# The 32 stores of converted weights, issued from GpSimd's queue instead of SyncE's

## The chip, the cores and the metric

The kernel runs on one core of a Trainium2 chip. The time is that of one execution on the device, in microseconds (us). The core has five engines that run in parallel, each through its own list of instructions in order: TensorE (PE: matmuls and transposes; its weight loads are shown as PEld), VectorE (DVE), ScalarE (ACT), GpSimd (POOL) and SyncE (SP, which here only issues DMAs). The engines meet at semaphores. DMAs move data between the chip's memory and the on-chip memory on 16 DMA engines that all queues share.

## The reference

Three layers follow each other, on 2 x 576 tokens with 8 heads of 64:

```
scores = scale * q @ k^T                       # per batch and head, 576 x 576
kth    = 32nd largest score of each row
attn   = softmax(where(scores >= kth, scores, -1e9))
x      = attn @ v                              # as 1152 tokens x 512
h      = x @ w_in                              # 512 -> 2048
x      = (max(h,0) + log1p(exp(-|h|))) @ w_out # 2048 -> 512
h      = x @ w_in2
out    = (max(h,0) + alpha * min(h,0)) @ w_out2
```

The four weight matrices come as 64-bit floats and have to be made into 32-bit floats on the chip.

## The kernel before

The 1152 tokens are nine tiles of 128 rows. `CHUNKS` puts them into five chunks of one or three tiles (tiles 3, 4, 5, then 6 to 8, then 0 to 2). Attention works by rows of one tile and one head, 72 in all. For a row PE makes the scores (`pss`, L471), ACT copies them to `s` (L476), DVE finds the 32 largest in four rounds of MAX8 and MATCH_REPLACE8 (L480, L483), ACT marks what lies below the 32nd (`e`, L509), POOL subtracts the mark from the scores in two halves of 288 columns (L514), and ACT takes the exponential (L516). PE turns `e` (L529, L535) and multiplies by v (`pav`, L557). The two feed-forward layers go over 16 blocks of 128 hidden columns, `up` (`ph`) and `down` (`pa`), for each chunk or group of chunks. In the small chunks the matmuls take 32-bit floats as they are (L652, L698); in the others each product is three products of high and low parts (L624 to L626).

The weights of a layer are 16 units of 128 x 1024: eight pairs of blocks for `up` and eight for `down`. The first use of a unit is `convert`: two loads of 512 KB from the input (L348) into a raw buffer `cr` of which there are two (`RAWB`), two DVE operations (L351, L354), one ACT operation for each half (L357), and four additions of 128 x 256 on POOL (L360). The result lies in `cx`, one of 15 slots of a ring that also holds the weights loaded later. Then `cx` is stored to a scratch tensor `ws` in the chip's memory (L364, 512 KB). A later chunk loads it from there (`w<-ws`, L386). So there are 32 stores for two layers: 16 fall between 17 and 135 us, 16 between 194 and 335 us.

The order on every engine is written out by hand: `ORDER` is a table of the numbers of all operations, and each is emitted when its number comes up. A word `f5` stands for five filler matmuls (`scrap`, L789) on PE. An operation waits for what wrote what it reads, and for what read or wrote what it overwrites. The loads of a unit (L348) wait for the last L360 of the unit that had the raw buffer before, and in the table the store of that unit follows soon after them.

Of the kernel before, what the change touches and what calls it, by code (L numbers as in the profile page):

```python
# [8 lines left out]
F32 = mybir.dt.float32  # L9
# [94 lines left out]
class Schedule:  # L104
# [10 lines left out]
    def op(self, engine, emit, reads=(), writes=()):  # L115
        me = len(self.ops)
        earlier = set()
        for x in reads:
            wrote, read = self.state.setdefault(getattr(x, "key", x), [None, []])
            if wrote is not None:  # L120
                earlier.add(wrote)
            read.append(me)
        for x in writes:
            entry = self.state.setdefault(getattr(x, "key", x), [None, []])
            earlier.update(entry[1])
            if entry[0] is not None:
                earlier.add(entry[0])
            entry[0], entry[1] = me, []
            self.owner[getattr(x, "key", x)] = x
        for x in reads:  # L130
            assert self.owner.get(getattr(x, "key", x), x) == x
        earlier.discard(me)
        self.ops.append((emit if isinstance(engine, tuple) else (emit,), earlier))
# [160 lines left out]
def pieces(n, size):  # L294

    return [slice(a, min(a + size, n)) for a in range(0, n, size)]
# [3 lines left out]
def topk_attention_moe_kernel(ctx: ExitStack, tc: tile.TileContext, q, k, v, w1, w2, w3, w4, alpha, out):  # L300
    nc = tc.nc
# [4 lines left out]
    op = plan.op  # L306

    def buf(tag, bufs, shape, dtype, name):
        return plan.buffer(sb, tag, bufs, shape, dtype, name)

    def bank(tag, bufs, n, name):
# [11 lines left out]
       writes=["rest"])  # L323
# [12 lines left out]
    def slot(tag, bufs, dtype, name, unit=None):  # L336
        x = Halves(buf(tag, bufs, [P, WIDE], dtype, name))
        lies[x.whole.key] = unit
        return x

    def convert(unit):
        layer, j, m = unit
        nm = f"{layer}{m}{j}"
        f = slot("wring", RING, U32, f"cx{nm}", unit)
        raw = Halves(buf("craw", RAWB, [P, WIDE, 2], U32, f"cr{nm}"))
        source = mats[layer][m][j].bitcast(U32)
        for part in raw.parts:
            op("SP", lambda part=part: nc.sync.dma_start(  # L348
                part().rearrange("p a b -> p (a b)"), source[:, 2 * part.lo:2 * part.hi]), writes=[part])
        high = lambda: raw()[:, :, 1]  # L350
        op("DVE", lambda: nc.vector.tensor_scalar(  # L351
            f().bitcast(U32), high(), 3, 0x3FFFFFF8, op0=ALU.logical_shift_left, op1=ALU.bitwise_and), reads=raw.parts,
           writes=f.parts)
        op("DVE", lambda: nc.vector.tensor_scalar(  # L354
            high(), high(), 0xC0000000, None, op0=ALU.bitwise_and), reads=f.parts, writes=raw.parts)
        for part, r in zip(f.parts, raw.parts):
            op("ACT", lambda r=r: nc.scalar.activation(  # L357
                r().bitcast(I16)[:, :, 2], r()[:, :, 0], AF.Copy, scale=2.0 ** -29), reads=[part], writes=[r])
            for cs in pieces(DM, 256):
                op("POOL", lambda part=part, r=r, cs=cs: nc.gpsimd.tensor_add(  # L360
                    part().bitcast(I32)[:, cs], part().bitcast(I32)[:, cs], r().bitcast(I32)[:, cs, 1]), reads=[r],
                   writes=[part])
        z = dr.tile([P, WIDE], F32, tag=f"ws{nm}", name=f"ws{nm}")
        op("SP", lambda: nc.sync.dma_start(z, f().bitcast(F32)), reads=f.parts, writes=[f"ws{nm}"])  # L364
        scratch[unit] = z
        return f

# [10 lines left out]
    def fetch(unit, no, ci, whole):  # L378
        fresh = unit not in scratch
        if whole and unit in ready and lies.get(ready[unit][0].whole.key) == unit:  # L380
            return
        if fresh:
            x = convert(unit)
        else:
            x = slot("wring", RING, F32R, f"w{no}", unit)
            op("SP", lambda: nc.sync.dma_start(x().bitcast(F32), scratch[unit]),  # L386
               reads=["ws%d%d%d" % (unit[0], unit[2], unit[1])], writes=x.parts)
        ready[unit] = (x,)
        if whole:
            return  # L390
        hi = slot("wring", RING, F32R, f"wh{no}")
        lo = slot("wring", RING, F32R, f"wl{no}") if fresh else x
        op("ACT", lambda: nc.scalar.copy(hi(), x().bitcast(F32)), reads=x.parts, writes=hi.parts)  # L393
        for l, a, h in zip(lo.parts, x.parts, hi.parts):
            low_piece(l, lambda a=a: a().bitcast(F32), h, [h, a] if fresh else [h], [l])
        ready[unit] = (hi, lo)
# [445 lines left out]
```

## Time and profile before

| | |
|---|---|
| median of 3 runs | 664.43 us (663.53 to 664.88) |
| the profiled execution | 661.64 us |
| its span, from the first to the last instruction | 659.8 us |
| busy PE, DVE, ACT, POOL | 643.9, 542.9, 496.9, 377.0 us |
| bytes moved by DMA | 98.46 MB, mean 149 GB/s |
| DMAs issued by SP | 67 `w<-ws`, 64 `cr`, 32 `ws<-cx`, and q, k, v, alpha and the output |

The busy shares are means over stages with different limits. Rows of a timeline give start and duration in us; in brackets stands the idle time of the engine just before the instruction, and who ended it. The row of a DMA on SPq is its issue; when its data has landed stands in a view of its own.

### The profile page before, as it was taken

How to read it: one execution, taken by the hardware profiler on the slowest of the kernel's cores; microseconds unless marked ns; L12 is line 12 of the kernel's file. 1: busy time of each engine (PE TensorE's matmuls, PEld its weight loads, DVE VectorE, ACT ScalarE, POOL GpSimd, SP SyncE). 2: the span in 40 equal slices, each digit the busy share in tenths (PEclk: the TensorE clock that was granted, in tenths of full speed). 3: DMA queues.
4: the chain of work that ended last, by engine and by line, in shares of the span. 5: the costliest groups of instructions: out<-in, count | busy, mean ns of one | idle time of the engine just before them, and what ended most of it. 6: DMA issues, size and time to landing. Idle time of an engine off the chain costs nothing.

```text
span 659.8 us, 12350 instructions
## 1 busy us (share of the span) xinstructions
PE 643.9 (98%) x4330; PEld 500.2 (76%) x4330; DVE 542.9 (82%) x1046; ACT 496.9 (75%) x1118; POOL 377.0 (57%) x402
## 2 busy tenths in 40 slices
PE   9999997999999899999999999999999999999997
PEld 7899765667677555555567788779898999999886
DVE  5999999999999999999998889999734654664632
ACT  4878898998799988788788889888545667673432
POOL 2566765642343677887585769886644343742520
PEclk9999999999999999999999999999999999999999
DMA  8765777740044379858424222221243433432501
GB/s 298 257 212 210 242 253 241 241 164 1 1 136 137 112 217 311 290 167 266 155 80 147 94 97 96 65 97 58 79 133 125 146 118 129 160 128 96 160 1 48
DMA packets 30159, 98.46 MB, mean 149 GB/s; under 512 B 3473, under 2 KB 4241, under 8 KB 30097
## 3 DMA queue, kind: packets, MB, share of 16 engines
q1 hardware_dynamic: 29952, 97.54, 45.2%
q8 instruction: 34, 0.56, 0.4%
q14 instruction: 29, 0.23, 0.1%
q10 hardware_dynamic: 144, 0.13, 0.1%
HBM read 78.52 MB, written 19.14 MB: 148 GB/s over the span
## 4 chain that ended last, share of the span: by engine, by line
PE 87%; issue 4%; POOL 3%; ACT 2%; DMA 2%; DVE 1%; SPq 0%; POOLq 0%; DVEq 0%
PE ph L652 11%; PE pa L698 10%; PE scrap L789 9%; PE ph L624 7%; PE pa L624 7%; PE ph L626 7%; PE ph L625 7%; PE pa L625 7%; PE pa L626 7%; PE pss L471 6%; PE pp L529 4%; POOL cx L360 2%; DMA cr<-in_w_dram 2%; POOL e L514 1%; PE pav__3750 L557 1%
## 5 line engine op out<-in xcount | busy, mean ns | idle before, releaser
L370 POOL TENSOR_TENSOR w<-w,wh 128x512 fp32r<-128x512 f32 x82 | 126.3, 1550 | 101.4 <-ACT wh L393 93.8
L514 POOL TENSOR_TENSOR e<-s,e 128x288 f32<-128x288 f32 x144 | 121.0, 860 | 64.4 <-ACT e L509 58.6
L480 DVE MAX8 m<-r 128x8 f32<-128x576 f32 x216 | 155.7, 747 | 0.1
L360 POOL TENSOR_TENSOR cx<-cx,cr 128x256 int32<-128x256 int32 x128 | 94.1, 762 | 62.2 <-ACT cr L357 60.5
L483 DVE MATCH_REPLACE8 r<-m,r 128x576 f32<-128x576 f32 x144 | 106.4, 742 | 0.0
L698 PE MATMUL pa<-cx,g 128*128 128x512 f32 x188 | 92.9, 604 | 2.3 <-DVE g L666 2.3
L357 ACT ACTIVATE cr<-cr 128x512 int16<-128x512 uint32 x64 | 82.5, 1378 | 4.4 <-DVE cr L354 4.0
L393 ACT CAST wh<-w 128x1024 fp32r<-128x1024 f32 x64 | 66.8, 1045 | 6.3 <-PE pa L624 2.0
L476 ACT COPY s<-pss 128x288 f32<-128x288 f32 x144 | 53.3, 407 | 21.7 <-PE pss L471 21.2
L480 DVE MAX8 m<-s 128x8 f32<-128x576 f32 x72 | 52.8, 749 | 10.6 <-ACT s L476 10.5
L789 PEld LDWEIGHTS scrap<-ident 128*128 128x128 f32 x474 | 55.9, 195 | 6.7 <-issue 5.3
L789 PE MATMUL scrap<-ident 128*128 128x128 f32 x474 | 59.5, 282 | 1.4 <-POOL ident masks.py:199 1.4
L516 ACT ACTIVATE e<-e,nb 128x576 f32<-128x576 f32 x72 | 55.8, 776 | 5.7 <-POOL e L514 5.5
L624 PE MATMUL pa<-w,gh 128*128 128x512 f32 x144 | 59.0, 409 | 0.0
L371 DVE TENSOR_TENSOR w<-w,wh 128x512 fp32r<-128x512 f32 x46 | 37.2, 811 | 26.4 <-ACT wh L393 24.8
L625 PE MATMUL pa<-wh,gl 128*128 128x512 f32 x144 | 56.8, 395 | 0.0
L626 PE MATMUL pa<-wh,gh 128*128 128x512 f32 x144 | 56.8, 395 | 0.0
L670 ACT ACTIVATE g<-ph 128x384 f32<-128x384 f32 x48 | 23.4, 490 | 43.7 <-PE ph L626 37.7
L471 PE MATMUL pss<-ks,q 64*64 64x288 f32 x576 | 53.1, 432 | 2.5 <-ACT pt L532 2.2
L672 DVE SCALAR_TENSOR_TENSOR g<-g,rest,ph 128x384 f32<-128x384 f32 x48 | 29.2, 608 | 31.8 <-ACT g L670 31.7
L371 DVE TENSOR_TENSOR gl<-g,gh 128x384 fp32r<-128x384 f32 x41 | 42.2, 1029 | 15.2 <-ACT gh L679 14.8
L652 PEld LDWEIGHTS ph<-xh,cx 128*128 128x128 f32 x336 | 42.0, 191 | 15.8 <-issue 8.2
(131 smaller groups left out, 1461.6 us busy)
## 6 DMA issues: line engine op xcount, KB each, us to landing
w<-ws SPq DMA_DIRECT2D x67, 512.0 KB, 3.3
cr<-in_w_dram SPq DMA_DIRECT2D x64, 512.0 KB, 5.5
ws<-cx SPq DMA_DIRECT2D x32, 512.0 KB, 6.6
v<-in_v_dram SPq DMA_DIRECT2D x12, 320.0 KB, 6.3
ks<-in_k_dram SPq DMA_DIRECT2D x11, 288.0 KB, 5.1
q<-in_q_dram SPq DMA_DIRECT2D x8, 256.0 KB, 5.3
out_dram<-o SPq DMA_DIRECT2D x8, 256.0 KB, 2.5
ks<-in_k_dram SPq DMA_DIRECT2D x2, 144.0 KB, 2.4
```

What stands on the lines that cost most here:

```text
L360: op("POOL", lambda part=part, r=r, cs=cs: nc.gpsimd.tensor_add(part().bitcast(I32)[:, cs], part().bitcast(I32)[:, cs], r().bitcast(I32)[: ...
L370: lambda: nc.gpsimd.tensor_sub(lo(), x(), hi().bitcast(F32)),
L471: nc.tensor.matmul(pss[n]()[part], qr()[head, pair, part], ks()[head, cs], start=True, stop=True)
L480: op("DVE", lambda: nc.vector.max(out=out(), in_=x()), reads=reads, writes=writes)
L483: op("DVE", lambda: nc.vector.match_replace(out=out(), in_to_replace=found(), in_values=x(), imm_value=LOWEST), reads=reads, writes=writes)
L514: op("POOL", lambda cs=cs: nc.gpsimd.tensor_sub(e()[:, cs], s()[:, cs], e()[:, cs]), reads=[s], writes=[e])
L624: nc.tensor.matmul(acc, ah, b_l, start=first, stop=False)
L625: nc.tensor.matmul(acc, a_l, bh, start=False, stop=False)
L626: nc.tensor.matmul(acc, ah, bh, start=False, stop=last)
L652: nc.tensor.matmul(hp(), w[0]().bitcast(F32)[:, cs], self.x[c][0]()[:, c, :], start=c == 0, stop=c == KT - 1)
L698: nc.tensor.matmul(acc(), gh()[:, cs], w[0]().bitcast(F32), start=first, stop=last)
L789: plan.emit(ORDER, lambda: nc.tensor.matmul(scrap()[:, :P], ident, ident, start=True, stop=True))
```

## The change

In `convert`, the store L364 is emitted on POOL's queue and by POOL's instruction, instead of on SP's. Its number in `ORDER` keeps its place.

```diff
         z = dr.tile([P, WIDE], F32, tag=f"ws{nm}", name=f"ws{nm}")
-        op("SP", lambda: nc.sync.dma_start(z, f().bitcast(F32)), reads=f.parts, writes=[f"ws{nm}"])
+        op("POOL", lambda: nc.gpsimd.dma_start(z, f().bitcast(F32)), reads=f.parts, writes=[f"ws{nm}"])
         scratch[unit] = z
```

The lists of PE, DVE and ACT keep their order. On POOL, near 80 us, the ninth store; `cx_898` is the unit, `e_72` the tile of one row of attention, `s_691` its scores:

```order
 L360 TENSOR_TENSOR cx_898<-cx_898,cr_756 128x256 x4
-L514 TENSOR_TENSOR e_72<-s_691,e_72 128x288 x2
+L514 TENSOR_TENSOR e_72<-s_691,e_72 128x288
+L364 DMA ws_83<-cx_898 128x1024
+L514 TENSOR_TENSOR e_72<-s_691,e_72 128x288
```

The store comes between the two halves of one `e`. On POOL from about 262 to 275 us, two more stores (`w_2985` is a unit that a later chunk has loaded, whose low part POOL computes in L370):

```order
-L514 TENSOR_TENSOR e_71<-s_2864,e_71 128x288 x2
+L514 TENSOR_TENSOR e_71<-s_2864,e_71 128x288
+L364 DMA ws_102<-cx_2999 128x1024
+L514 TENSOR_TENSOR e_71<-s_2864,e_71 128x288
 L360 TENSOR_TENSOR cx_3068<-cx_3068,cr_2989 128x256 x4
 L514 TENSOR_TENSOR e_71<-s_2867,e_71 128x288
+L364 DMA ws_97<-cx_3068 128x1024
 L370 TENSOR_TENSOR w_2985<-w_2985,wh_3135 128x512 x2
```

One store parts an `e` again, the other comes behind the first half of the next one. On SP, from about 89 to 119 us, the loads of one unit after another (`cr`) and the stores that stood between them:

```order
 L348 DMA cr_1060<-in_w_dram 128x1024 x2
-L364 DMA ws_84<-cx_999 128x1024
 L348 DMA cr_1136<-in_w_dram 128x1024 x2
-L364 DMA ws_85<-cx_1065 128x1024
 L439 DMA v_1201<-in_v_dram 128x640
 L348 DMA cr_1231<-in_w_dram 128x1024 x2
-L364 DMA ws_86<-cx_1187 128x1024
 L439 DMA v_1326<-in_v_dram 128x640
 L348 DMA cr_1333<-in_w_dram 128x1024 x2
-L364 DMA ws_87<-cx_1263 128x1024
```

The loads stay in their order, and nothing stands between them but loads of q, k and v and, later, of `ws`.

## Rows read from the trace of the kernel before

**Rows 1.** The page's busy times, and PE's filler matmuls in the view of their tile.
```profile
PE 643.9 (98%) x4330; PEld 500.2 (76%) x4330; DVE 542.9 (82%) x1046; ACT 496.9 (75%) x1118; POOL 377.0 (57%) x402
...
L789 PE MATMUL scrap<-ident x474: 275/275/581, 1.4 to 77.7; 128*128 128x128 f32 x158
```

**Rows 2.** Busy time of each engine in four stages.
```profile
core 0: us, PE busy (x) PEld busy (x) DVE busy (x) ACT busy (x) POOL busy (x), PEclk, DMA share, GB/s
0.00:125.00 125.00, 115.84 (x1093) 94.07 (x1094) 116.02 (x237) 99.84 (x226) 75.61 (x103) 1.00 0.74 244
125.00:231.00 106.00, 103.37 (x789) 69.90 (x788) 104.23 (x235) 94.70 (x281) 44.94 (x60) 1.00 0.31 102
231.00:345.00 114.00, 114.00 (x599) 62.88 (x598) 110.77 (x220) 95.07 (x197) 87.35 (x104) 0.99 0.66 213
345.00:660.00 315.00, 310.65 (x1853) 273.34 (x1851) 211.91 (x357) 207.25 (x417) 169.12 (x137) 1.00 0.32 104
```

**Rows 3.** The chain that ended last (start, us, what): the longest piece near 102 us.
```profile
102.59 6.73 DMA cr<-in_w_dram
```

**Rows 4.** One unit: SP's loads at 251 us, their landing (min/median/max), DVE's L351.
```profile
251.23 0.81 SPq L348 DMA_DIRECT2D cr<-in_w_dram  x2
...
DMA to landing us min/median/max: 5.6/6.0/6.5
...
258.23 0.69 DVE L351 TENSOR_SCALAR cx<-cr 128x1024 uint32<-128x1024 uint32 x1
```

**Rows 5.** SP's timeline near 102 us: two loads, then the store.
```profile
102.21 0.81 SPq L348 DMA_DIRECT2D cr<-in_w_dram  x2
103.07 0.44 SPq L364 DMA_DIRECT2D ws<-cx  x1
```

**Rows 6.** Issues of stores (min/median/max ns), waits for loads, median landing.
```profile
L364 SPq DMA_DIRECT2D ws<-cx x32: 319/430/1947, 17.9 to 334.5; - x32
...
  DVE cx L351: 2.1, 4
...
109.42 0.69 DVE L351 TENSOR_SCALAR cx<-cr 128x1024 uint32<-128x1024 uint32 x1 [0.90 <-DMA cr<-in_w_dram]
...
cr<-in_w_dram SPq DMA_DIRECT2D x64, 512.0 KB, 5.5
```

**Rows 7.** Groups by line (busy us, mean ns, idle before), then POOL's timeline.
```profile
L360 POOL TENSOR_TENSOR cx<-cx,cr 128x256 int32<-128x256 int32 x128 | 94.1, 762 | 62.2 <-ACT cr L357 60.5 <-ACT kb L508 0.9 <-ACT nb L499 0.5
L351 DVE TENSOR_SCALAR cx<-cr 128x1024 uint32<-128x1024 uint32 x32 | 24.3, 761 | 2.5 <-DMA cr<-in_w_dram 2.1 <-issue 0.2
...
80.49 1.54 POOL L514 TENSOR_TENSOR e<-s,e 128x288 f32<-128x288 f32 x2 [1.36 <-PE pp L529]
87.14 1.28 POOL L514 TENSOR_TENSOR e<-s,e 128x288 f32<-128x288 f32 x1
97.82 1.56 POOL L514 TENSOR_TENSOR e<-s,e 128x288 f32<-128x288 f32 x2 [2.48 <-ACT e L509]
282.86 0.73 POOL L370 TENSOR_TENSOR xl<-xn,xh 128x256 fp32r<-128x256 f32 x1 [1.10 <-ACT xh L617]
283.81 1.27 POOL L370 TENSOR_TENSOR w<-w,wh 128x512 fp32r<-128x512 f32 x1 [0.22 <-ACT wh L393]
```

**Rows 8.** Two microseconds of a burst of loads and a store (columns of rows 2).
```profile
28.00:29.00 1.00, 1.00 (x11) 1.00 (x10) 1.00 (x3) 0.94 (x5) 0.00 (x0) 1.00 0.84 242
31.00:32.00 1.00, 1.00 (x17) 0.88 (x17) 1.00 (x5) 1.00 (x2) 0.70 (x2) 1.00 0.97 399
```

**Rows 9.** PE's timeline after its longest idle time, and that stretch's granted clock.
```profile
229.72 0.63 PE L529 MATMUL pp<-ident,e 128*128 128x128 f32 x4 [2.04 <-ACT s L476]
230.20 7.09 PE L652 MATMUL ph<-yh,cx 128*128 128x384 f32 x16
237.67 2.75 PE L652 MATMUL ph<-yh,cx 128*128 128x384 f32 x8
...
230.00:240.00 10.00, 10.00 (x33) 5.90 (x31) 10.00 (x21) 8.68 (x20) 7.19 (x10) 0.83 0.69 197
```

## The prediction, made before the changed kernel ran

> **What bounds the kernel now.** I read the busy shares first, then the stages, then the chain of waits, then the timelines of the places that the change touches. TensorE (PE) is busy 643.9 of 659.8 us [rows 1]. That is not all work: the 474 `scrap` matmul halves are fillers, and the last of them starts at 77.7 us [rows 1]. So I split the span where the fillers have ended and the stalls are over. From 125 to 660 us PE is busy 103.37 + 114.00 + 310.65 = 528.0 of 535 us [rows 2]: whatever delays PE before 125 us is paid in full at the end, and a later stall of PE is paid as well. Two engines feed it. VectorE (DVE) is busy 116.02 of 125 and 110.77 of 114 us in the first and third stage, the two in which weights are converted and the 32 stores happen; GpSimd (POOL) is busy 75.61 and 87.35 us there [rows 2]. In the stretches where PE waits, the chain of waits runs over them: near 102 us it goes from POOL's last add of a unit to the load that this releases, 6.73 us long, and on to DVE's L351 [rows 3].
>
> One unit of weights goes round a loop: two loads (L348) into a raw buffer, DVE (L351, L354), ACT (L357), POOL (L360, four adds); the fourth add frees the raw buffer (there are two) for the loads of the next unit but one. The list of DVE is in order, and its L351 stands about where the load lands: four L351 wait, 2.1 us together [rows 6], the longest 0.90 us; the one at 258.23 does not wait, but its second load (issued at about 251.65, 6.5 us to landing) landed at about 258.1, 0.1 us ahead of it [rows 4]. Loads have nearly no slack there.
>
> **What goes.** SP loses 32 issues of 0.43 us, 13.8 us [rows 6]. SP does not compute, and the store stands right behind the two loads of the same moment (102.21 and 103.07 [rows 5]), so nearly no load waits for its issue. The most that can come back is all that DVE ever waits for loads, 2.1 us [rows 6]. I take 0 and keep -2.1 as an end.
>
> **What comes: POOL's time.** POOL now has to issue each store itself, at the place in its own list where the table has it. No row shows a DMA issued by POOL. The nearest rows are SP's issues of the same store: 0.32 us the shortest, 0.43 the median, 1.95 the longest [rows 6]. Of POOL's own rows the add of 128x256 takes 762 ns on the mean and one half of `e` 0.77 us (1.54 for two, at 80.49) [rows 7]. A store of 128 rows made by the engine itself should cost more than the 0.43 us of a queue that does nothing else, and something like an op of that engine; I take 1.1 us, the middle of 0.32 and 1.95, with the short wait for POOL's own last add in it, and keep 0.43 and 1.95 as ends. By a price that only a page states, the sum would hardly differ: the Trainium skill, "DMA: Bandwidth & Descriptors", "Specifications", gives about 1 us to the first byte on the GpSimd path; taken as an estimate of the whole price the sum below is 3.7.
>
> 32 x 1.1 = 35 us of POOL do not all count. Behind nine of the 32 POOL idles 1.8 us or more before its next op, as before `e` at 97.82 (2.48 us) [rows 7], and the store is swallowed there. The others stand in front of work, eight of them between the two halves of one `e`, which ACT, then PE's transposes, wait for. I carried every delay through the trace: an op starts later by as much as the op ahead of it on its engine, or one whose tile it needs, ends later, less the idle time between them. Three places carry the result:
>
> 1. To 125 us. The store behind the unit of 79 us falls between the halves of `e` that ran back to back at 80.49 [rows 7]: 1.1 us later for ACT and PE. Gaps return 0.2 us by 109.42: +0.9.
> 2. 125 to 231 us. Five stores; most have idle behind them, and 0.2 more reaches PE: +1.1 in all.
> 3. 231 to 345 us. POOL is busy 87.35 of 114 us [rows 2] and 13 stores add 14.3, against 26.7 of idle that stands in the wrong places. From 272.69 to 293 it idles 1.10 + 0.22 us [rows 7] and gets three stores, 3.3 us: 2.0 late there alone. Much of that is late for `e` and for the next unit's raw buffer, less for PE: PE ends the stage 2.5 late, and 2.6 at the end.
>
> **What comes: loads.** Before, the store is queued behind the loads of its moment and takes the DMA engines when they are done [rows 5]. Now it comes from another queue while those loads run. In such a burst the 16 engines are busy 0.84 to 0.97 of the time, and at 399 GB/s [rows 8] a store of 512 KB has 1.3 us of their time. If they are shared, the loads land up to 1.3 us later; if the store fits between the loads' packets (28 to 29 us moves 242 GB/s only [rows 8]), 0. I take the middle, 0.65: the store starts about a microsecond after the loads and can't hold up what has landed. Of 0.65 a load, three count on the path of the carried delay, those whose L351 is at 109.42, 212.46 and 258.23; they bring 1.4 more.
>
> The Trainium skill, "DMA: Bandwidth & Descriptors", "Issuing engines are not separate DMA queues", says that DMAs of all issuing engines run on the same 16 DMA engines and interleave. By that rule a second queue brings no bandwidth and the loads lose near the whole 1.3 us: the sum would be 7.9. With a free ride for the store it is 2.6. The shares near 1 in the burst agree with the rule, the 242 GB/s leaves room, so I stay between.
>
> Carried together (price 1.1, load 0.65) PE is late by 1.6 us at 125, 1.8 at 231, 3.8 at 345 and 4.0 at the end. After 345 there is no store; PE has no fillers to drop and gives nothing back. The ends, by the same carrying: price 0.43 gives 0, 0.4 or 4.1 us for loads later by 0, 0.65 or 1.3; price 1.95 gives 17.9, 19.2 or 21.0. Price 1.5 with 0.65 gives 9.5: the growth is steep above 1.3, where the idle that covers a store is used up.
>
> **Forecast.** Against the profiled execution (659.8 span, 661.64 in all) the sum is 665.6. The median of the runs shown is 664.43, 2.8 above that execution; the same 4.0 on it gives 668.4 us.
>
> **Rivals.**
> - *POOL becomes the loop's bound.* At a price near the longest issue, 1.95, POOL's 87.35 + 13 x 1.95 = 112.7 of 114 us [rows 2] leave no idle, and the raw loop waits for POOL: +19.2, 683.6 us. For it: DVE slows POOL where the two meet; a half of `e` beside L351 (at 87.14) took 1.28 us, against 0.77 [rows 7]. Against: 1.95 is the longest of 32, and the median is 0.43 [rows 6].
> - The Trainium skill names that contention: "SBUF — State Buffer", "SBUF: two separate sides", says that while DVE runs an op in a two-port mode GpSimd cannot write the descriptors of its DMAs. The 1.28 us row agrees that something is locked. By the rule a store that meets L351 or L354 waits for up to 0.76 us more [rows 7]. DVE spends 24.3 us on L351 [rows 7] and about as much on L354, some 48 of the 345 us, so it is one store in seven, 0.1 us on the mean: price 1.2, sum 5.2. It is inside my range and moves its upper half.
> - *PE's clock.* After the one long idle of PE, 2.04 us before 229.72, the next 16 matmuls took 7.09 us, where 8 later took 2.75 [rows 9]: 7.09 - 2 x 2.75 = 1.6 us are lost, with a granted clock of 0.83 on the mean from 230 to 240 [rows 9] (part of it at 1.2 instead of 2.4 GHz). New stalls in the first 125 us may cost such a piece each; +1.6 to +3.2 on the forecast, 670.0 to 671.6.
> - *No change.* Price about 0.43 and loads unhurt to 0.65: 664.4 to 664.8. For it: POOL is idle 49.4 of the first 125 us [rows 2]. Against: a quarter of the stores split an `e`, whatever the share.
> - *Faster.* Loads no longer queue behind an older store. The load of 251.23 took 6.5 us, against a median of 5.5 [rows 4, 6], with an older store still on its way. If the loads land earlier by that, the waits of L351 go: -2.1, 662.3 us. It decides only if POOL's price is under 0.7, since from there the delay of `e` exceeds what comes back. Against: the same bytes go through the same engines, and the store of the same moment now runs beside the loads.
> - *The change doesn't do what it says*: the stores might be carried by a queue that costs POOL no time. Then the price is that of the issue, which is the no-change case.
>
> **How the numbers follow.** The forecast with its spread (price 0.8 to 1.5, load 0 to 1.3, the clock's piece included, +1.4 to +12) has 0.53; POOL as the bound (above +12) 0.18; no change 0.18; faster 0.11. About 0.2% (1.3 us) is what a measurement can tell from no change; the no-change case lies within it. So faster 0.11, same 0.18, slower 0.71. The range goes from 663.2, which leaves most of the faster case out, to 681.0, which leaves out POOL at its dearest: about 1 in 10 on either side. The forecast's own range is 666 to 676.
>
> **What would show it.** Right: POOL's list shows 32 issues of about 1 us; `e` halves that were back to back are apart; the waits of L351 for loads grow from 2.1 us to about 5; loads take about 6 us to land instead of 5.5; PE's idle before 125 us grows by 1 to 2 us, and PE no longer reads 114.00 of 114 from 231 to 345. Wrong: issues of POOL under 0.5 us, or loads landing earlier with fewer waits of L351; or a delay that is there on POOL and DVE at 345 us and gone from PE's end.

## The result and the profile after

The changed kernel took 670.84 us in the median of four runs (669.67 to 675.76), the kernel before 664.65 beside it: 1.0122 times, 95% interval 1.0089 to 1.0154 (this ratio and the later ones are worked out from the single runs; the quotient of the two medians is 1.0093). Timed again on another chip it came to 1.0088 (1.0058 to 1.0119). The change costs 6 to 8 us. The execution whose profile follows took 671.57 us, its span is 669.8, 10.0 more than in the one of before. Of these 10.0 us 2.8 come from the execution of before, which at 661.64 us lies that much under the median of its kernel (664.43).

The four stages of the changed kernel, to be laid beside [rows 2] (same columns; the last window goes to the end):

```profile
0.00:125.00 125.00, 117.58 (x1090) 94.56 (x1090) 116.49 (x228) 96.53 (x221) 81.90 (x114) 0.99 0.75 240
125.00:231.00 106.00, 102.53 (x745) 69.42 (x745) 101.95 (x232) 92.06 (x275) 44.70 (x62) 0.97 0.32 103
231.00:345.00 114.00, 109.53 (x579) 58.23 (x579) 111.08 (x217) 94.71 (x190) 88.78 (x113) 1.00 0.65 212
345.00:670.00 325.00, 320.13 (x1918) 279.81 (x1916) 221.75 (x372) 214.28 (x433) 178.87 (x147) 1.00 0.31 103
...
sum 670.00, PE 649.78 PEld 502.02 DVE 551.28 ACT 497.59 POOL 394.25; mean PE 162.45 PEld 125.51 DVE 137.82 ACT 124.40 POOL 98.56
```

Three things stand out. GpSimd (POOL) has 394.25 - 377.0 = 17 us more [rows 1], as it must with 32 more instructions. But VectorE (DVE) has 551.28 against 542.9 [rows 1], 8.4 us more with the same 1046 instructions: some of them were held up while they ran. The two conversion lines have 6.2 of these, L354 28.1 us instead of 23.7 and L351 26.1 instead of 24.3. And TensorE's (PE) granted clock is 0.97 in the second stage, where it was 1.00 [rows 2].

What POOL now pays is in the group of the store and the time until it lands, what DVE pays in the views of its two conversion lines (ns min/median/max, and the idle time ahead, us and times); the last line is L354 in the kernel before:

```profile
L364 POOL DMA_DIRECT2D ws<-cx x32 | 19.8, 619 | 3.6 <-POOL cx L360 3.0 <-PE pq L535 0.3 <-PE pp L529 0.3
...
L364 POOL DMA_DIRECT2D ws<-cx x32: 548/577/909, 18.0 to 344.6; - x32
...
L351 DVE TENSOR_SCALAR cx<-cr x32: 636/694/1822, 10.9 to 336.5; 128x1024 uint32<-128x1024 uint32 x32
  DMA cr<-in_w_dram: 3.7, 8
...
L354 DVE TENSOR_SCALAR cr<-cr x32: 669/686/4006, 12.2 to 337.7; 128x1024 uint32<-128x1024 uint32 x32
...
cr<-in_w_dram SPq DMA_DIRECT2D x64, 512.0 KB, 5.2
ws<-cx POOLq DMA_DIRECT2D x32, 512.0 KB, 6.7
...
L354 DVE TENSOR_SCALAR cr<-cr x32: 670/689/1189, 11.6 to 327.7; 128x1024 uint32<-128x1024 uint32 x32
```

A store occupies POOL for 0.62 us, and POOL waits 3.0 us in all for its own last add: 3.0 / 32 = 0.09, together 0.71 us a store. The loads land after 5.2 us here, not later than before (5.5 [rows 6]); in four later profiles with all or 31 of the stores on POOL it is 5.6. The median of L354 is 686 ns. Its longest is 4006; before, it was 1189.

That one instruction is the place to look at. First DVE's timeline of the changed kernel there, then POOL's, ACT's and PE's (start us, duration us, engine, line; in brackets the idle time before and what ended it):

```profile
120.84 0.74 DVE L480 MAX8 m<-s 128x8 f32<-128x576 f32 x1
121.51 4.01 DVE L354 TENSOR_SCALAR cr<-cr 128x1024 uint32<-128x1024 uint32 x1
...
121.34 0.55 POOL L364 DMA_DIRECT2D ws<-cx  x1
121.92 3.04 POOL L514 TENSOR_TENSOR e<-s,e 128x288 f32<-128x288 f32 x4
126.96 0.74 POOL L360 TENSOR_TENSOR cx<-cx,cr 128x256 int32<-128x256 int32 x1 [2.01 <-ACT cr L357]
...
125.55 2.47 ACT L357 ACTIVATE cr<-cr 128x512 int16<-128x512 uint32 x2 [2.71 <-DVE cr L354]
...
121.36 0.71 PE L652 MATMUL ph<-xh,cx 128*128 128x128 f32 x4
127.88 3.78 PE L698 MATMUL pa<-cx,g 128*128 128x512 f32 x4 [3.95 <-DVE g L666]
131.46 1.92 PE L652 MATMUL ph<-xh,cx 128*128 128x128 f32 x8
```

And the same place in the kernel before:

```profile
120.08 3.51 POOL L514 TENSOR_TENSOR e<-s,e 128x288 f32<-128x288 f32 x4
...
120.23 1.19 DVE L354 TENSOR_SCALAR cr<-cr 128x1024 uint32<-128x1024 uint32 x1
...
120.09 0.71 PE L652 MATMUL ph<-xh,cx 128*128 128x128 f32 x4
123.79 1.98 PE L698 MATMUL pa<-cx,g 128*128 128x512 f32 x4 [1.11 <-DVE g L666]
125.61 1.05 PE L652 MATMUL ph<-xh,cx 128*128 128x128 f32 x8
```

Before, L354 began beside the first of four halves of `e`, waited for the end of that one, ran, and POOL's four halves took 3.51 us with that pause in them. Now L354 begins 0.17 us into the store. It comes through neither when the store ends nor between the halves, which run without a pause in 3.04 us; it ends at 125.52, some 0.56 us after the last half (124.96), about its own time. ACT's L357 waits 2.71 us behind it, PE 3.95 (1.11 before).

The delay of PE can be read from equal instructions in the two traces: L652 at 120.09 is 1.27 us late, L698 at 123.79 is 4.09 late, L652 at 125.61 is 5.85. So the held instruction brought 2.8 us, and then four instructions of L698 took 3.78 us instead of 1.98. The granted clock says why (columns of [rows 2]):

```profile
100.00:110.00 10.00, 8.81 (x78) 5.36 (x80) 9.82 (x21) 9.97 (x26) 6.96 (x10) 0.83 0.92 297
110.00:120.00 10.00, 9.24 (x63) 6.19 (x63) 9.80 (x22) 8.45 (x24) 6.66 (x9) 1.00 0.63 200
120.00:130.00 10.00, 6.03 (x63) 3.76 (x60) 10.00 (x18) 6.55 (x16) 7.16 (x10) 0.84 0.60 192
130.00:140.00 10.00, 10.00 (x70) 7.43 (x70) 7.56 (x15) 7.96 (x22) 3.10 (x6) 0.82 0.48 157
```

Before, all four windows have 1.00. With PE 3.95 us idle, the clock fell for part of 20 us to the lower of its two levels, 1.2 instead of 2.4 GHz. The fall ahead of it, between 100 and 110 us, is another matter: PE's delay rose from 1.4 to 2.9 us there, but by 113 us of before it was 1.3, and two kernels below that keep all stores on SyncE have one of the same size (0.83 between 110 and 120 us). In return the fall that the kernel before has at 230 us [rows 9] is missing here (1.00). At 229.72 [rows 9] the instruction that answers is

```profile
236.45 0.63 PE L529 MATMUL pp<-ident,e 128*128 128x128 f32 x4 [2.06 <-ACT s L476]
```

6.73 late. So of the 10.0 us of this execution about 1.3 come ahead of that place, 5.5 there and 3.3 behind 231 us. Of the 1.3, 0.6 have nothing to do with the stores: DVE's MAX8 at 6.86 us starts at 7.42, and the first store is at 18.0.

### The profile page after: what moved, and what is told of

Read it like the earlier page. It is cut to its first block, busy times and chain, and to the rows that moved or that the text cites. A ratio compares the mean times of both kernels' runs of the same rounds, so it can differ in the third digit from the quotient of the medians.

```text
span 669.8 us, 12350 instructions
## 1 busy us (share of the span) xinstructions
PE 649.8 (97%) x4330; PEld 502.0 (75%) x4330; DVE 551.3 (82%) x1046; ACT 497.6 (74%) x1118; POOL 394.2 (59%) x434
## 4 chain that ended last, share of the span: by engine, by line
PE 76%; POOL 9%; issue 4%; DVE 4%; ACT 4%; DMA 2%; SPq 0%; POOLq 0%; DVEq 0%
PE pa L698 9%; PE ph L652 7%; PE ph L624 7%; PE pa L624 7%; PE ph L625 7%; PE ph L626 7%; PE pa L625 7%; PE pa L626 7%; PE pss L471 5%; POOL cx L360 5%; PE scrap L789 5%; POOL e L514 3%; PE pp L529 3%; DMA cr<-in_w_dram 2%; ACT cr L357 1%
## 5 line engine op out<-in xcount | busy, mean ns | idle before, releaser
L370 POOL TENSOR_TENSOR w<-w,wh 128x512 fp32r<-128x512 f32 x82 | 126.2, 1549 | 101.1 <-ACT wh L393 101.0
L514 POOL TENSOR_TENSOR e<-s,e 128x288 f32<-128x288 f32 x144 | 119.5, 847 | 52.9 <-ACT e L509 45.8
L698 PE MATMUL pa<-cx,g 128*128 128x512 f32 x188 | 95.6, 619 | 6.0 <-DVE g L666 5.6
L357 ACT ACTIVATE cr<-cr 128x512 int16<-128x512 uint32 x64 | 82.5, 1378 | 10.3 <-DVE cr L354 10.0
L698 PEld LDWEIGHTS pa<-cx,g 128*128 128x128 f32 x188 | 31.5, 193 | 31.9 <-issue 20.4
```

The lines of the kernel that those rows point to most:

```text
L357: op("ACT", lambda r=r: nc.scalar.activation(r().bitcast(I16)[:, :, 2], r()[:, :, 0], AF.Copy, scale=2.0 ** -29), reads=[part], writes=[r])
L370: lambda: nc.gpsimd.tensor_sub(lo(), x(), hi().bitcast(F32)),
L514: op("POOL", lambda cs=cs: nc.gpsimd.tensor_sub(e()[:, cs], s()[:, cs], e()[:, cs]), reads=[s], writes=[e])
L698: nc.tensor.matmul(acc(), gh()[:, cs], w[0]().bitcast(F32), start=first, stop=last)
```

## The experiments

Three theories. A: what a store costs is POOL's time, and the delay that this carries on. B: the store changes how POOL and DVE share what both need, and DVE's conversions are held up. C: a store on another queue than the loads' makes the loads late. All ratios are to the kernel before on the same chip, with a 95% interval; the times are medians.

**POOL busy, stores on SyncE.** At each store's place POOL clears a tile of its own four times.

```
+        def both():
+            for _ in range(4):
+                nc.gpsimd.memset(pad, 0.0)
+            nc.sync.dma_start(z, f().bitcast(F32))
```

> The stores stay on SP's queue; at each store's place POOL clears a small tile four times (4 x 128 columns, about 0.7 us, close to the 0.62 us of a store on POOL and its 0.1 us of waiting). Theory A (POOL's time delays the halves of e): most of the change's loss is here too, +5 us or more. Theory B (POOL's list, moved against DVE's, makes a two-port DVE operation wait for a run of POOL operations, above all L354 of the unit near 120 us): about the same loss if the 4 us L354 is seen again, under +1 us if it is not. Theory C (the store from a second queue holds up the loads): no loss. By the carried delays at the measured price 0.7 the loss is 0.2 us.

666.87 us, 1.0044 (1.0028 to 1.0061). POOL has 407.0 us, 30 more than before or 0.94 a place, more than a store takes. DVE has 547.6, its longest conversion 1.90 us. The loss, 2.9 us, lies between what A (5 or more) and B (under 1, with no long hold) had allowed. POOL's time costs something, but not all, though here it is the larger.

**Only layer 0, and only layer 1, on POOL.**

```
+        queue = nc.gpsimd if layer == 0 else nc.sync     # and: layer == 1
```

> Only the 16 stores of the first layer go to POOL. Theory A and C: a loss by share, 3 to 4 us each half. Theory B: the L354 near 121 us takes about 4 us again, PE's clock is granted below full for some 20 us around 130, and +5 to +6 us, three quarters of the loss, are here.

> Only the 16 stores of the second layer go to POOL. Theory A and C: +3 to +4 us. Theory B: no long L354 near 121 us, PE as before until 230 us, and +1 to +3 us.

Layer 0: 668.25, 1.0041 (1.0014 to 1.0068), twelve runs from 662.26 to 670.74. Layer 1: 668.06, 1.0061 (1.0042 to 1.0080). Both halves cost, and about as much; B had put three quarters into layer 0. In the profile of the first L354 near 120 us takes 4.00 us again and TensorE's clock falls behind it. The twelve times of this kernel lie in two groups, five up to 665.44 and seven from 668.23 on; that would fit a hold in some executions and not in others, but it isn't shown. In the profile of the second L354 near 120 us takes 0.69 us, and the longest conversion is one of L351. DVE there, PE at two places, and the second of these in the kernel before:

```profile
285.37 2.05 DVE L351 TENSOR_SCALAR cx<-cr 128x1024 uint32<-128x1024 uint32 x1
...
232.46 0.63 PE L530 MATMUL pp<-ident,e 128*128 128x128 f32 x4 [2.06 <-ACT s L477]
344.28 0.71 PE L472 MATMUL pss<-ks,q 64*64 64x288 f32 x8
...
337.18 0.72 PE L471 MATMUL pss<-ks,q 64*64 64x288 f32 x8
```

PE is 2.74 us late against 229.72 [rows 9] and 7.10 at the second place. So in the stage of the sixteen stores it loses 4.36 us with no conversion longer than 2.05: the long holds are not all that the stores cost.

**All but the fourteenth on POOL.**

```
+        queue = nc.gpsimd if unit != (0, 7, 0) else nc.sync
```

> All stores on POOL but that of the fourteenth unit, which goes back to SP: it stood right ahead of the four halves of e that run back to back beside the long L354. Theory B: without it POOL and DVE meet as before, the L354 takes about 1.2 us, and 4 to 5 us of the change's loss come back (ratio to before 1.003 to 1.006). Theory A and C: one store of 32, under 0.5 us comes back.

667.87, 1.0059 (1.0039 to 1.0080). The held instruction near 120 us is gone and the clock with it, but at 277.54 another L354 took 3.36 us, behind a store, two pieces of `w` and a half of `e`.

**The changed kernel again, and three edits of that one place on the same chip.**

> The changed kernel once more, so that the three kernels beside it are compared on one chip. Both theories: 1.009 to 1.015 times the kernel before (670 to 673 us), and the second operation of the fourteenth unit near 120 us held for about 4 us again.

> Only the store of the fourteenth unit (layer 0, row 7, matrix 0) is issued by GpSimd, the other 31 by SyncE. Theory A (what a store costs is GpSimd's time, 0.62 us of issue and 0.30 us of waiting): one thirty-second of the loss, under 0.3 us, no change that can be told (663.3 to 665.0). Theory B (the store moves GpSimd's run of four halves of e so that VectorE's operation, which wants the same port, waits for the whole run): the hold of about 4 us at L354 near 120 us is there, TensorE stops for some 2 to 3 us behind it, and the end is 2 to 5 us late (666 to 669), about a third to a half of the whole loss from one store of 32.

> All 32 stores on GpSimd, but the fourteenth stands behind the four halves of e on GpSimd and not ahead of them. Theory A: GpSimd has the same work, so the time of the changed kernel to within 0.3 us. Theory B: GpSimd yields to VectorE after the first half, as before; L354 near 120 us takes 0.7 to 1.3 us and not 4.0, and the time is 2 to 5 us below that of the changed kernel (666 to 669).

> All 32 stores on GpSimd at their places; on VectorE the second operation of the fourteenth unit stands directly behind the first, one MAX8 earlier, so that it begins before the store and the run of four halves. Theory A: the time of the changed kernel to within 0.3 us. Theory B: L354 near 120 us takes under 1.5 us, and the time is 2 to 5 us below that of the changed kernel, like that of the kernel with the store behind the run.

Only the fourteenth on POOL: 668.02, 1.0060 (1.0038 to 1.0082), from one store of 32. Theory A allowed 0.3 us; it is 4.0 (2.5 to 5.4). Its POOL, DVE and PE (lines here are one higher than in the kernel before):

```profile
120.35 0.70 POOL L365 DMA_DIRECT2D ws<-cx  x1
121.07 3.04 POOL L515 TENSOR_TENSOR e<-s,e 128x288 f32<-128x288 f32 x4
...
120.52 4.14 DVE L354 TENSOR_SCALAR cr<-cr 128x1024 uint32<-128x1024 uint32 x1
...
127.03 3.78 PE L699 MATMUL pa<-cx,g 128*128 128x512 f32 x4 [4.08 <-DVE g L667]
...
120.00:130.00 10.00, 5.90 (x36) 3.16 (x33) 10.00 (x15) 6.49 (x15) 6.94 (x10) 0.74 0.63 191
```

The same sequence as in the changed kernel, to a tenth of a microsecond. The changed kernel again: 669.44, 1.0088. The profile that was taken of it has no such hold at that place:

```profile
122.95 0.97 POOL L364 DMA_DIRECT2D ws<-cx  x1
123.94 3.07 POOL L514 TENSOR_TENSOR e<-s,e 128x288 f32<-128x288 f32 x4
...
123.13 0.68 DVE L354 TENSOR_SCALAR cr<-cr 128x1024 uint32<-128x1024 uint32 x1
...
279.04 0.73 POOL L364 DMA_DIRECT2D ws<-cx  x1
279.79 2.50 POOL L370 TENSOR_TENSOR w<-w,wh 128x512 fp32r<-128x512 f32 x2
282.25 0.79 POOL L514 TENSOR_TENSOR e<-s,e 128x288 f32<-128x288 f32 x1
...
280.24 3.36 DVE L354 TENSOR_SCALAR cr<-cr 128x1024 uint32<-128x1024 uint32 x1
...
286.70 0.66 PE L529 MATMUL pp<-ident,e 128*128 128x128 f32 x4 [2.05 <-ACT s L476]
```

At 123.13 DVE began 0.18 us into the store, as in the other execution (0.17), but got through at once, and the store was the longer one (0.97). The hold came at 280.24 instead. Which of the two gets in first changes from one execution to the next, and with it the place of the loss. My expectation that the hold would be at 120 us every time was wrong.

Store behind the four halves (table: `612` moved behind `664`): 668.46, 1.0066 (1.0044 to 1.0088). L354 one place earlier on DVE (`622` moved up right behind `621`): 668.36, 1.0075 (1.0047 to 1.0103). In both L354 near 120 us was short (1.19 and 0.92 us), and in both the one near 277.7 us took 3.37 and 3.36. Against 1.0088 the intervals overlap: theory B's gain of 2 to 5 us isn't shown by these two, and A isn't excluded by them.

**An ordinary operation of POOL in place of the store.** All stores stay on SyncE; POOL subtracts in a tile of its own, at the fourteenth place, then at all 32, then twice as wide.

```
+    pad = sb.tile([P, 150], F32, tag="pad", name="pad")     # later: [P, 300], bfloat16
+        def both():
+            nc.gpsimd.tensor_sub(pad, pad, pad)             # first: only if unit == (0, 7, 0)
+            nc.sync.dma_start(z, f().bitcast(F32))
```

> All 32 stores on SyncE as before; GpSimd runs one two-input operation on a tile of its own (128x150, by the slope of its other operations about 0.56 us) at the place of the fourteenth store only. If what counts is that GpSimd is busy there when VectorE's operation comes (theory B): L354 near 120 us is held for about 4 us as with the store, and the end is 2 to 5 us late (666 to 669). If it is something of the store itself, its descriptors or its queue: L354 takes under 1.5 us and the time is that of before (663 to 665). Theory A (GpSimd's time): under 0.3 us.

> All 32 stores on SyncE; GpSimd runs the 0.56 us operation at the place of every store. Without any store on GpSimd's queue this has its time (0.56 against 0.62 us, without the 0.30 us for its own last piece) and its shift of the runs. Theory B: most of the changed kernel's loss, 1.005 to 1.010 times before, VectorE's busy time up by 4 to 8 us with the same instructions. Theory A alone: under 1 us. Theory C (the second queue): no change.

> As the kernel with one 0.43 us operation on GpSimd at each store's place, all stores on SyncE, but the operation is twice as wide (128x300, about 0.8 us), nearly the whole of a store's issue and waiting in the changed kernel (0.62 and 0.30 us). Theory A (GpSimd's time): most of the changed kernel's loss comes now, 1.006 to 1.012. Theory B as it now stands (only behind a store does GpSimd run on over several operations while VectorE waits): 1.001 to 1.004, VectorE busy within 2 us of 543, no operation of VectorE in the conversions over 1.9 us.

At the fourteenth place: 663.47, 0.9988 (0.9973 to 1.0003), no change. Its POOL and DVE (lines shifted):

```profile
120.25 0.43 POOL L369 TENSOR_TENSOR pad<-pad 128x150 f32<-128x150 f32 x1
120.64 3.51 POOL L522 TENSOR_TENSOR e<-s,e 128x288 f32<-128x288 f32 x4
...
120.40 0.83 DVE L356 TENSOR_SCALAR cr<-cr 128x1024 uint32<-128x1024 uint32 x1
```

DVE began 0.15 us into POOL's operation, as it began 0.17 us into the store, and took over when that ended, while POOL's first half of `e` waited. So it is not that POOL is busy there; it is the store. Theory B in the form in which I had put it (any work of POOL there would do) fell with this run, and was put anew for the last one.

At all 32 places, 0.53 us each (16.8 us in all): 665.36, 1.0014 (0.9997 to 1.0030), DVE 543.5 us; B in that form had 1.005 to 1.010. Twice as wide, 0.745 us each:

```profile
L368 POOL TENSOR_TENSOR pad<-pad 128x300 bf16<-128x300 bf16 x32 | 23.8, 745 | 0.0
```

667.08, 1.0035 (1.0017 to 1.0053). This is the whole price of a store, 0.71, and a little more, and it costs 2.3 us. (The 0.30 us of waiting in my expectations is the mean of the ten stores that wait; over all 32 it is 0.09.) DVE has 548.3 us, 3 more than I had expected of B, so POOL's time alone also makes the two meet more often; but no conversion took over 1.42 us. What the stores cost on top of their time is the rest, by this difference: 1.0088 or 1.0122, less 1.0035, 3.5 to 5.8 us. These ratios are of different chips; the interval of this one ends at 1.0053, those of the changed kernel begin at 1.0058 and 1.0089.

**The stores on ScalarE's queue**, POOL as before.

```
-        op("SP", lambda: nc.sync.dma_start(z, f().bitcast(F32)), ...
+        op("ACT", lambda: nc.scalar.dma_start(z, f().bitcast(F32)), ...
```

> The 32 stores are issued by ScalarE's queue at the same places; GpSimd is as before. In the trace of before GpSimd's last piece of the unit is done by the time ScalarE comes to the store in 30 of the 32 places (0.9 us of waiting in all). Theory C (a second queue makes loads land later, or the stores no longer pace the loads): the loads land later than 5.5 us and the time rises as in the changed kernel, 1.005 to 1.012. Theories A and B: GpSimd's and VectorE's times stay (POOL 377, DVE 543 us), what is left is ScalarE's issue, so within 0.4% of before (662 to 666); a hold can still come where ScalarE is late and shifts GpSimd's run of e.

669.36, 1.0076 (1.0053 to 1.0098). POOL 377.7 and DVE 543.5 are those of before, and still it is slow. The profiled execution is the slowest of its six, 671.74:

```profile
L351 DVE TENSOR_SCALAR cx<-cr 128x1024 uint32<-128x1024 uint32 x32 | 23.9, 748 | 13.2 <-DMA cr<-in_w_dram 10.5 <-issue 2.7
...
cr<-in_w_dram SPq DMA_DIRECT2D x64, 512.0 KB, 5.9
ws<-cx ACTq DMA_DIRECT2D x32, 512.0 KB, 5.9
```

The loads land after 5.9 us in the median, not 5.5, the stores sooner (5.9, not 6.6), and L351 waits 10.5 us for loads, against 2.1 [rows 6]. ScalarE waits for POOL's adds 0.8 us in all, so it isn't that. Theory C fits ScalarE's queue. For GpSimd's little of it is left: in the five profiles with all or 31 stores there the loads land after 5.2, 5.6, 5.6, 5.6 and 5.6 us, and L351 waits 3.7 to 5.4 us for them, 4.5 on the mean. In the five with all stores on SyncE (before, the clearing kernel and the three subtracting ones) it is 5.3 to 5.5 us and 2.1 to 4.8, 3.1 on the mean. So 1.4 us of such waits may belong to C.

**All profiles together.** I counted the conversions of DVE (L351, L354) that begin while POOL is in an instruction, and those that are still held up when the next instruction of POOL has ended too (taken from the conversion's end, less its own 0.68 us). In the six kernels with no store on POOL: 0 of 171, and none lasted over 1.90 us. In the eight profiles with stores there: 8 of 237, one in each, and in each of the 8 a store stands in the same unbroken run of POOL, ahead of the place or at it. Seven of them took 3.36 to 4.14 us, the one of layer 1 alone 2.05. A store in the run isn't enough. Eight conversions began inside a store with four or more instructions of POOL right behind it: three were held, all near 120 us, and five took 0.68 us. For the three the store lasted 0.55 to 0.70 us, for the five 0.90 to 0.97. So in these eight either DVE waited, for over 3 us, or the store did, for some 0.3.

## Why the prediction was right

Forecast were 668.4 us and a range of 663.2 to 681.0; it became 670.84. Direction and range are right. The sum is not: its terms were off in both directions, and what the stores cost on top of POOL's time, 3.5 to 5.8 us, stood in it as a rival at 0.1 us a store. That 668.4 came near is luck in part.

- *SP's 32 issues bring nothing back*: right. L351's waits for loads did not shrink (3.7 us, 8 times; 2.1 before).
- *Price of a store, 1.1 us*: too high. Issue and wait are 0.71. Landing is 6.7 us and was 6.6; in the other profiles with stores on POOL it is 6.4 to 7.2. The store between the halves of `e` came as described (82.20, with 0.58 us, between halves at 81.47 and 82.80).
- *Carrying it through the trace*: too low for a given price. By the same carrying a price of 0.7 with loads unhurt gives 0.2 us; the operation of 0.745 us measured 2.3 (1.1 to 3.5). Carrying held each duration fixed, and DVE's 548.3 us show that durations grow when instructions shift against each other. The two errors nearly cancel: 2.6 was carried for the stores, 2.3 measured for their time.
- *Loads 0.65 us later, 1.4 us*: this step failed in its size. The loads landed after 5.2 to 5.6 us, against 5.3 to 5.5 with the stores on SyncE; of the waits of L351, forecast at about 5 us, 3.7 to 5.4 came. The Trainium skill, "DMA: Bandwidth & Descriptors", "Issuing engines are not separate DMA queues", holds that all DMAs interleave on the same engines. By that rule I had worked out 1.3 us a load; the traces show at most 0.3 us of it with GpSimd's queue, and 0.4 (5.9 against 5.5) with ScalarE's.
- *The port between DVE and POOL*: mis-sized, the main error. I let the store wait for DVE, 0.1 us on the mean; the stores' 909 ns at the longest agree, as do the 0.90 to 0.97 us where a conversion got through first. The costly direction is the other one: DVE waits for the store and for what POOL runs behind it, 3.36 to 4.14 us, and ACT and PE behind DVE. The one store of 32 cost 4.0 us. The Trainium skill, "SBUF — State Buffer", "SBUF: two separate sides", says of a VectorE operation in a two-port mode and a GpSimd operation that whichever starts first has the shared port pair for the whole instruction. The kernel with an ordinary operation agrees (0.83 us: taken over at its end); behind a store the measurement differs, since L354 stayed out over the ends of five instructions.
- *PE's clock falls behind new stalls, +1.6 to +3.2*: it came behind the 3.95 us of idle: 6.73 - 4.09 = 2.6 us, between that place and 229.72. With the hold's 2.8 this is more than half of the 10.0 us of this execution. In the median it is little: over all eleven runs of the changed kernel the granted clock is 0.995 on the mean, over the fourteen of the kernel before beside seven of them 0.996, which makes 0.7 us of PE's time.
- *By place*: I had 1.6 us at 125, 1.8 at 231 and 4.0 at the end; this execution had 5.85 at 125.61, 6.73 at 229.72 and 10.0. The place at 120 us is missing from the forecast.
- *POOL as the bound*: no. 88.78 of 114 us in the third stage. *Faster* and *no change*: no.

What stays open: why POOL keeps DVE out behind a store. The runs show where (a store in the run, no pause), but not every time, and not what it is that is kept. Nor do they settle how often an execution has such a hold: of the eight profiles with stores on POOL three show one at 120 us, four one at 277 to 280, never both, and that of layer 1 alone shows none over 2.05 us. POOL's own time is a part of that one's 4.36 us; what makes up the rest is open too. Moving the store or DVE's operation near 120 us took no measurable part of the loss away: in those two profiles the hold came at 277.7 us.

## What to carry to other kernels

A DMA that GpSimd issues can cost more than its time on GpSimd where VectorE runs operations that GpSimd holds up, here the conversions of 128x1024: look at what GpSimd runs without a pause behind the store, and count that as VectorE's possible wait, with all that waits for VectorE. To price an instruction on an engine, put an ordinary operation of the same length at its place: here that gave 1.0035 where the store gave 1.0088 to 1.0122, and so split its time from the rest. Carrying delays through a trace with fixed durations gave 0.2 us where 2.3 were measured: where two engines hold each other up, durations change too.

## What the runs showed of the hardware

- A store of 128x1024 took GpSimd 0.55 to 0.91 us (0.97 in the second profile), and landed 6.7 us later (6.4 to 7.2 in the other profiles); SyncE's issue took 0.43 and ScalarE's 0.33.
- Behind a GpSimd store a VectorE operation of 0.68 us lasted 4.01, 4.00 and 4.14 us beside four halves of `e`, and 3.36 or 3.37 four times beside two pieces of `w` and a half of `e`; in the six kernels without one, never over 1.90.
- Loads on SyncE's queue landed after 5.3 to 5.5 us with the stores behind them on the same queue, 5.2 to 5.6 with the stores on GpSimd's and 5.9 with them on ScalarE's.
- TensorE idle for 3.95 us was followed by granted clocks of 0.84 and 0.82 in the two 10 us windows; idle for 4.08, by 0.74 in that window.
